# Block-sparse attention with a SwiGLU FFN: one dense batch instead of two, and block batches loaded by GpSimd-issued DMAs

## Chip, cores and metric

The kernel runs on one core of a Trainium2 chip. The metric is the time of one execution in microseconds on the device. The kernel before takes 307.14 us, the median of three runs (306.61 to 308.03). The profile comes from one further execution of 307.95 us, in which 306.2 us lie between the first and the last instruction (the span).

## What is computed

Four batches of eight heads, 768 tokens and head dimension 64 go through attention with a block mask, and the result through a gated FFN. The mask works on blocks of 32 tokens (24 per batch): a query block sees itself and its neighbours, the first and the last block, and three sampled blocks; the first and the last query block see everything.

```python
blk_i, blk_j = pos[:, None] // 32, pos[None, :] // 32
mask = (abs(blk_i - blk_j) <= 1) | (blk_i == 0) | (blk_j == 0) | (blk_i == 23) | (blk_j == 23)
for qb in range(24):
    for kb in sampled_blocks[qb]:
        mask[qb * 32:(qb + 1) * 32, kb * 32:(kb + 1) * 32] = True
attn = softmax(where(mask, q @ k.T / 8, -1e9)) @ v            # [4, 8, 768, 64]
x = attn, heads side by side                                   # [3072, 512]
xn = x / sqrt(mean(x * x) + 1e-6) * rms_g
out = (silu(xn @ w_gate) * (xn @ w_val)) @ w_out               # 512 -> 1536 -> 512
```

## The kernel before

**Two ways of attention.** Batches 0 and 1 are dense: all 768 x 768 scores of a head are computed, with the mask carried by 24 further rows of the contraction (88 = 64 + 24). Batches 2 and 3 are done by blocks: for each tile of four query blocks only the keys and values that the mask allows are gathered and multiplied. The work is cut into units of one to three tiles of 128 tokens (`UNITS`, L59 to L63). Batch 0 has units of 1, 1, 1 and 3 tiles, the others two units of 3. Tile 5 (`AT`) of a block batch holds the first and the last query block, which see everything, with the two blocks before the last.

**A dense unit.** `dk` (L322) computes scores, `dexp` (L343, ScalarE) the exponential, `dav` (L357) multiplies with the values, whose column 65 is ones and gives the row sum, and `dxo` (L369, L370, VectorE) divides by it. Batch 0's queries and keys are turned by TensorE (L301) and batch 1's by DMA transposes (`turn`, L288), after loads by SyncE (`load`, L275) and casts on VectorE (`fill`, `pad_v`).

**A block batch.** SyncE loads raw k, v (`load_kv`, L452, halves of 768 KB with two tokens side by side, in rows of 512 bytes) and q (`load_q`, L459, rows of 256 bytes) into three raw buffers. `fill_v`, `fill_k` and `fill_q` cast them to bf16, on GpSimd for batch 2. `turn_k` (L478) and `turn_q` (L504) are DMA transposes that SyncE issues. `store_v` (L508) writes the bf16 values to DRAM as rows `vrows`. For each tile, `kg_fixed` copies the neighbour and end blocks of the keys and `kg_sampled` (GpSimd, L146) the sampled ones, at columns that registers hold. `pair_v` (L570, L572, L578, SyncE) fetches the fixed value rows. `block_v` (L555) fetches each sampled block of 32 value rows by a DMA of its own: SyncE issues those of the first and second sample, ScalarE those of the third. Then come `qk` (L599) or, for tile 5, `qka` (L615), `exp` (L605) or `expa` (L623), `av` (L648) and `xo` (L658, L659). Registers are loaded once by `table_regs` (L435) on each engine that uses them.

**The FFN of a unit.** `sq`, `rsq` (L686, a power on GpSimd) and `xq` (L693) normalize. Units below `NPET` = 6 are turned by TensorE (`tr`, L704; `cp`), the later ones by a DMA transpose (`xt`, L715). Then for each slice `f` of the hidden dimension TensorE does gate and value (`proj`, L728), ScalarE a tanh (`th`, L737), and VectorE `uu` (L743) and `hp` (L754). TensorE ends with `yy` (L767), ScalarE or VectorE scale (`yo`, L777, L779), and SyncE stores (`so`, L789, L795). Weights come by DMAs that GpSimd issues and that cast to bf16 (`load_w` L248, `load_wo` L252).

**What sets the order.** A planner at the end of the function holds every piece of work as an `op` with a cost for each engine that may do it, dependencies, a priority and the buffers that it takes and gives back. It fixes one order for each engine ahead of time. Each engine then runs its list in order, so an instruction that waits holds up everything after it on its engine. Ops in `seq` keep the order given there. Buffers overlay one another: those of the block batches lie in storage that the dense batches have given back (keys `("old", i)`), so their release sets when block work may begin.

Of the kernel before, what the change touches and what calls it, by code (L numbers as in the profile page):

```python
# [16 lines left out]
def kernel(  # L17
# [32 lines left out]
    NR, NHP, NXN, NYO, NPET = NRND, 2, 2, 3, 6  # L50
    NSLOT, NAUG, NOPEN, NDB = 5, 2, 2, 2
    IXAT, RGAT = 36.0, 48.0
    NPT, NPA, NKG, NVG, NRAW = 4, 2, 2, 3, 3
# [4 lines left out]
    HD = NC * D // 2  # L58
    UNITS = [(0, 0, 1), (0, 1, 1), (0, 2, 1), (0, 3, 3)]  # L59
    UNITS += [(b, c, 3) for b in range(1, NDB) for c in (0, 3)]  # L60
    ND = len(UNITS)
    for b in range(NDB, B):
        UNITS += [(b, (5, 0, 1), 3), (b, (2, 3, 4), 3)]  # L63
    NU = len(UNITS)
    HG = [("h", 0 if u < 3 else u) for u in range(NU)]
    HO = [u if u < 3 else 0 for u in range(NU)]
# [9 lines left out]
    def bank16(n):  # L76
# [12 lines left out]
    VAC = const.tile([P, 2, H * NC, D + 2], BF16, name="VAC")  # L89
    VGC = const.tile([P, 6, VW], BF16, name="VGC")  # L90
# [6 lines left out]
    RAWD = list(A)  # L97
    RAWS = [RAWC[:, i * RB:(i + 1) * RB] for i in range(NRAW)]
    aug = [AUG[:, i] for i in range(NAUG)]
    va_ = [VAC[:, i] for i in range(2)]  # L100
    vfl = [t.rearrange("p m d -> p (m d)")[:, 0:6 * VW] for t in va_]
    VAUG = [t.rearrange("p (t c h d) -> p t c h d", t=NC // 2, c=2, h=H) for t in (vfl[0], PTC[:, 10240:10240 + 6 * VW])]
    rt_ = RAWC[:, NRAW * RB:].bitcast(BF16)
    VGB = [VGC, rt_[:, 0:6 * VW].rearrange("p (x w) -> p x w", w=VW),
           vfl[1].rearrange("p (x w) -> p x w", w=VW)]
    PD = [PTC[:, i * PDW:(i + 1) * PDW] for i in range(3)]
    PTB = [t.rearrange("p (h l x) -> p h l x", h=2, l=2) for t in [rt_[:, 6 * VW:6 * VW + 1024]] + [
        PTC[:, i * 1024:(i + 1) * 1024] for i in range(NPT - 1)]]
    PAB = [PTC[:, 3072 + i * 2048:3072 + (i + 1) * 2048].rearrange("p (l h x) -> p l h x", l=2, h=2) for i in range(NPA)]
    KTB = [t.rearrange("p (a s) -> p a s", a=NP) for t in (xs_[3], xs_[1])]  # L110
    QTB = [t.rearrange("p (a s) -> p a s", a=NP) for t in (xs_[4], PTC[:, 7168:7168 + NP * S])]
    KGB = [xs_[i].rearrange("p (x a s j c) -> p x a s j c", x=6, a=NP, s=4, j=16) for i in (0, 2)]
    KROW = AUG[:, 0].rearrange("p i e c x -> p (i e c x)").rearrange(
        "p (a c t x) -> p a c t x", a=NP, c=2, t=NC // 2)
    QROW = AUG[:, 1].rearrange("p i e c x -> p (i e c x)").rearrange("p (a n x) -> p a n x", a=NP, n=NC)
    kvv = [t.rearrange("b h (t p c) d -> b p (h t) (c d)", p=P, c=2) for t in (k, v)]
    qvv = q.rearrange("b h (n p) d -> b n p h d", p=P)
# [32 lines left out]
    zt = const.tile([P, VW], BF16, name="zt")  # L150
# [36 lines left out]
    nc.gpsimd.memset(zt[0:32, P:VW], 0.0)  # L187
# [9 lines left out]
    for t in va_:  # L197
        nc.vector.memset(t[:, :, D:D + 1], 1.0)
# [72 lines left out]
    def load(g, i):  # L271
        b, pr = divmod(g, NP)
        if i == 0:
            rawd[g] = RAWD[held["rawd", g][1]]
        nc.sync.dma_start(out=rawd[g][:, i], in_=(kv, qv, vv)[i][b, :, 2 * pr:2 * pr + 2, :])  # L275

    def fill(g, i, eng):
        copy(eng, aug[g % NAUG][:, i, :, :, 0:D],
             rawd[g][:, i].rearrange("p h (c d) -> p h c d", d=D))

    def pad_v(g, eng):
        b, pr = divmod(g, NP)
        src = rawd.pop(g) if b else A[g]
        copy(eng, va_[b][:, 2 * pr * NC:2 * (pr + 1) * NC, 0:D],
             src[:, 2].rearrange("p h (c d) -> p (h c) d", d=D))

    def turn(g):
        nc.sync.dma_start_transpose(  # L288
            out=X[g % NSLOT].rearrange("p i e (c t) -> p (i e c) t", t=P),
            in_=aug[g % NAUG].rearrange("p i e c r -> p (i e c r)"))  # L290
# [656 lines left out]
    def dep0(g0, b, c0, nt, kt, g):  # L947
        if b:
            return [("turn", g0)]
# [373 lines left out]
```

## Time and profile before

| | |
|---|---|
| median of the runs | 307.14 us (306.61 to 308.03) |
| the profiled execution, its span | 307.95 us, 306.2 us |
| TensorE busy in matmuls | 284.4 us (93%) |
| VectorE, ScalarE, GpSimd busy | 195.1, 175.2, 80.3 us |
| bytes moved by DMA | 48.50 MB, 158 GB/s over the span |
| packets: all, and under 512 bytes | 85,204 and 48,037 |
| hardware queue of SyncE (q1), share of 16 engines | 54.7% |
| GpSimd's software queue (q0), the same | 10.1% |

A busy time counts the instructions of an engine; registers, semaphores and the issuing of DMAs are not in it and appear under the engine's queue (SPq, ACTq, POOLq). The chain of waits goes back from the last instruction to what released it, step by step; a step on it is work that the end waited for. In a group such as `L728 ... x480 | 74.3, 294`, the numbers are the count, the busy us together and the mean ns of one; then follow the idle time of the engine just before and what ended it.

### The profile page before, as it was taken

The numbers are of one execution on the slowest core, as the hardware profiler recorded it, in microseconds if no ns is written. First come the engines' busy times: TensorE is split into PE (matmuls) and PEld (weight loads), VectorE is DVE, ScalarE is ACT, GpSimd is POOL, SyncE is SP. The second block draws the span as 40 slices with busy tenths as digits, with TensorE's granted clock in tenths as the row PEclk, the third lists the DMA queues.
The fourth block names the chain that finished last, engine by engine and source line by source line (L and its number), as shares of the span: only waits on it lengthen the run. The fifth ranks groups of instructions, "written<-read, shape, count | busy, mean of one in ns | idle before, by whom it ended". The sixth has DMA issues, their size and how long they took to land.

```text
span 306.2 us, 9818 instructions
## 1 busy us (share of the span) xinstructions
PE 284.4 (93%) x3838; PEld 183.4 (60%) x3838; DVE 195.1 (64%) x462; ACT 175.2 (57%) x290; POOL 80.3 (26%) x196
## 2 busy tenths in 40 slices
PE   8999989889999998999779699998699999999995
PEld 7899877666666664665445345564255655546543
DVE  6688896576756755877568435767177958807700
ACT  4899874468888785368554226877065424413322
POOL 4648100010024615119754200755041000100000
PEclk9999999999999999999999979999989999999999
DMA  7999999864799996783987973333754400060032
GB/s 218 364 242 157 203 268 323 182 229 80 119 267 266 182 308 161 159 239 87 263 196 187 195 157 97 90 84 89 166 127 135 92 36 2 0 156 0 1 98 109
DMA packets 85204, 48.50 MB, mean 158 GB/s; under 512 B 48037, under 2 KB 81318, under 8 KB 85158
## 3 DMA queue, kind: packets, MB, share of 16 engines
q1 hardware_dynamic: 76946, 41.63, 54.7%
q0 software_dynamic: 5792, 4.72, 10.1%
q10 hardware_dynamic: 2420, 1.53, 2.0%
q8 instruction: 30, 0.49, 0.6%
q14 instruction: 16, 0.13, 0.1%
HBM read 36.70 MB, written 8.02 MB: 146 GB/s over the span
## 4 chain that ended last, share of the span: by engine, by line
PE 67%; DMA 14%; DVE 8%; issue 5%; SPq 2%; ACT 2%; ACTq 1%; DVEq 0%
PE PS L728 33%; PE PS L767 15%; PE PS L322 7%; PE PS L357 4%; DMA RAWC<-in_v_dram 4%; PE PS L648 3%; DMA XC<-AUG 2%; DMA RAWC<-in_k_dram 2%; PE PS L301 2%; DMA VGC<-vrows 2%; DVE uu L743 2%; PE PS L599 2%; DMA xn<-xq 1%; DVE hp L754 1%; ACT th L737 1%
## 5 line engine op out<-in xcount | busy, mean ns | idle before, releaser
L737 ACT ACTIVATE th<-PS 128x384 bf16<-128x384 f32 x96 | 46.5, 492 | 81.9 <-PE PS L728 37.5
L743 DVE SCALAR_TENSOR_TENSOR uu<-th,PS 128x384 bf16<-128x384 bf16 x96 | 52.4, 551 | 49.4 <-ACT th L737 47.1
L728 PE MATMUL PS<-xn,wg 128*128 128x384 bf16 (+1 forms) x480 | 74.3, 294 | 7.3 <-DVE uu L743 4.2
L343 ACT ACTIVATE PTC<-PS 128x768 bf16<-128x768 f32 x92 | 70.4, 815 | 14.0 <-PE PS L322 13.8
L728 PE MATMUL PS<-xn,wv 128*128 128x384 bf16 (+1 forms) x480 | 77.9, 297 | 0.1
L767 PE MATMUL PS<-wo,hp 128*128 128x512 bf16 (+1 forms) x300 | 71.4, 376 | 4.1 <-DVE uu L743 4.1
L754 DVE TENSOR_TENSOR hp<-uu,PS 128x384 bf16<-128x384 bf16 x96 | 52.0, 551 | 16.8 <-PE PS L728 14.7
L728 PEld LDWEIGHTS <-wg 128*128 128x128 bf16 x480 | 40.7, 98 | 31.4 <-issue 9.0
L146 POOL COPY XC<-XC 128x128 bf16 x132 | 39.3, 371 | 62.6 <-PE PS L599 35.7
L728 PEld LDWEIGHTS <-wv 128*128 128x128 bf16 x480 | 40.5, 98 | 23.9 <-issue 1.9
L767 PEld LDWEIGHTS <-hp 128*128 128x128 bf16 x300 | 29.0, 99 | 32.4 <-issue 6.2
L322 PE MATMUL PS<-XC 88*128 88x128 bf16 (+1 forms) x288 | 42.6, 276 | 0.6 <-ACT PTC L343 0.6
L322 PEld LDWEIGHTS <-XC 88*128 88x128 bf16 x288 | 22.2, 100 | 7.8 <-issue 0.9
L357 PE MATMUL PS<-VAC,PTC 128*128 128x65 bf16 x552 | 21.1, 193 | 0.2 <-DVE XO L370 0.2
L357 PEld LDWEIGHTS <-PTC 128*128 128x128 bf16 x552 | 20.0, 97 | 2.0 <-issue 0.3
L777 ACT ACTIVATE yo<-PS 128x512 f32<-128x512 f32 (+1 forms) x16 | 9.1, 571 | 20.2 <-PE PS L767 20.1
L146 POOL CAST AUG<-RAWC 128x768 bf16<-128x768 f32 (+3 forms) x12 | 11.6, 973 | 30.1 <-DMA RAWC<-in_k_dram 25.7
L693 DVE SCALAR_TENSOR_TENSOR xq<-XO,rs,gB 128x512 bf16<-128x512 f32 x24 | 18.5, 792 | 0.2 <-POOL rs L686 0.2
L686 POOL TENSOR_TENSOR rs<-ms,nhalf 128x1 f32<-128x1 f32 (+1 forms) x6 | 4.3, 714 | 47.8 <-DVE ms L675 47.8
L605 ACT ACTIVATE PTC<-PS 128x1024 bf16<-128x1024 f32 x15 | 15.2, 1022 | 1.6 <-PE PS L599 1.1
L648 PEld LDWEIGHTS <-PTC 128*32 128x32 bf16 x736 | 8.1, 97 | 8.7 <-issue 7.4
L599 PEld LDWEIGHTS <-XC 64*128 64x128 bf16 x480 | 7.5, 93 | 6.9 <-issue 5.8
(112 smaller groups left out, 225.1 us busy)
## 6 DMA issues: line engine op xcount, KB each, us to landing
out_dram<-yo SPq DMA_DIRECT2D x21, 256.0 KB, 2.0
RAWC<-in_k_dram SPq DMA_DIRECT2D x4, 768.0 KB, 5.7
RAWC<-in_v_dram SPq DMA_DIRECT2D x4, 768.0 KB, 10.6
RAWC<-in_q_dram SPq DMA_DIRECT2D x12, 256.0 KB, 5.3
RAWC<-in_v_dram SPq DMA_DIRECT2D x7, 384.0 KB, 6.5
RAWC<-in_k_dram SPq DMA_DIRECT2D x6, 384.0 KB, 6.6
wg<-in_moe_w_gate_dram POOLq DMA_DIRECT2D x4, 384.0 KB, 6.9
wv<-in_moe_w_val_dram POOLq DMA_DIRECT2D x4, 384.0 KB, 7.9
```

The source lines that it names most:

```text
L146: nc.gpsimd.tensor_copy(out=out, in_=in_)
L322: nc.tensor.matmul(out=s_[:, e, j * w:(j + 1) * w], lhsT=x[0:KQ, 0, e, jt * P:(jt + 1) * P], rhs=x[0:KQ, 1, e, c0 * P:c0 * P + w], start=T ...
L343: nc.scalar.activation(out=pts[u, pr][:, g * kt:(g + 1) * kt].rearrange("p j e w -> p e j w"), in_=s_[:, :, 0:kt * w].rearrange("p e (j w) ...
L357: nc.tensor.matmul(out=o_[:, t, e, :], lhsT=pt[:, jt, e, t * P:(t + 1) * P], rhs=va[:, (2 * pr + e) * NC + jt, 0:D + 1], start=(jt == 0), ...
L605: nc.scalar.activation(out=t_.rearrange("p h l x -> p (h l x)"), in_=tiles.pop(("s", b, n, pp)).rearrange("p h l x -> p (h l x)"), func=AF ...
L648: nc.tensor.matmul(out=o_[32 * i:32 * i + 32, a, :], lhsT=l_, rhs=r_, start=i not in begun, stop=k_ == last[i], tile_position=(0, 32 * i), ...
L693: nc.vector.scalar_tensor_tensor(out=xqs[u][:, t, :], in0=xos[u, t].rearrange("p h d -> p (h d)"), scalar=mss[u][:, t:t + 1], in1=gB, op0= ...
L728: nc.tensor.matmul(out=p_[:, j, :].rearrange("p (t w) -> p t w", w=P), lhsT=w_[:, c, f_ * P:(f_ + 1) * P], rhs=xns[u][:, :, c, :], start=( ...
L737: nc.scalar.activation(out=t_, in_=tiles["gp", u, f], func=AF.Tanh, scale=0.5)
L743: nc.vector.scalar_tensor_tensor(out=t_, in0=tiles.pop(("th", u, f)), scalar=1.0, in1=tiles.pop(("gp", u, f)), op0=ALU.add, op1=ALU.mult)
L754: nc.vector.tensor_tensor(out=hps[u][:, f * fg:(f + 1) * fg, :], in0=tiles.pop(("uu", u, f)), in1=tiles.pop(("vp", u, f)), op=ALU.mult)
L767: nc.tensor.matmul(out=tiles["yp", u, t, h], lhsT=hps[u][:, f, t * P:(t + 1) * P], rhs=wo[:, f, x], start=(f == 0), stop=(f == NF - 1))
```

## The change

Batch 1 is done by blocks like batches 2 and 3 (`NDB` 2 to 1), and everything that loaded, cast, turned and multiplied a dense batch above 0 goes. Units of the block batches are 1, 2, 1, 2 tiles in batch 1, 1, 2, 3 in batch 2 and 3, 3 in batch 3; units below 8 are turned by TensorE. The block batches' tokens lie in their natural order: k, v and q are all loaded in halves of 768 KB with rows of 256 bytes, and key copies read runs of 32 neighbouring columns. GpSimd issues these loads, behind the weights. SyncE gathers the first sample of each block, ScalarE the second and the third; their row numbers are packed two to a register. All fixed key copies are VectorE's. There are four value buffers instead of three. Register loads may start at 36 us of the plan (48 before). The core of the diff:

```diff
-    NR, NHP, NXN, NYO, NPET = NRND, 2, 2, 3, 6
-    NSLOT, NAUG, NOPEN, NDB = 5, 2, 2, 2
-    IXAT, RGAT = 36.0, 48.0
-    NPT, NPA, NKG, NVG, NRAW = 4, 2, 2, 3, 3
+    NR, NHP, NXN, NYO, NPET = NRND, 2, 2, 3, 8
+    NSLOT, NAUG, NOPEN, NDB = 5, 2, 2, 1
+    IXAT, RGAT = 31.0, 36.0
+    NPT, NKG, NVG, NRAW = 5, 2, 4, 3
+    SPLIT = (((5,), (0,1), (2,),( 3, 4)), ((5,), (0, 1), (2, 3, 4)), ((5, 0, 1), (2, 3, 4)))
-    UNITS += [(b, c, 3) for b in range(1, NDB) for c in (0, 3)]
-        UNITS += [(b, (5, 0, 1), 3), (b, (2, 3, 4), 3)]
+        UNITS += [(b, ns, len(ns)) for ns in SPLIT[b - NDB]]
...
-    kvv = [t.rearrange("b h (t p c) d -> b p (h t) (c d)", p=P, c=2) for t in (k, v)]
-    qvv = q.rearrange("b h (n p) d -> b n p h d", p=P)
+    kvv = [t.rearrange("b h (t p) d -> b p (h t) d", p=P) for t in (k, v, q)]
...
-    REGS = {"POOL": [("k", 0, 16), ("k", 16, 32), ("k", 32, 2 * NS)], "SP": [("v", 0, 16), ("v", 16, 32), ("v", 32, 2 * NS)],
-            "ACT": [("v", 2 * NS, 2 * NS + 11), ("v", 2 * NS + 11, 3 * NS)]}
+    REGS = {"POOL": [("k", 0, 16), ("k", 16, 32), ("k", 32, 2 * NS)],
+            "DVE": [("k", 0, 16), ("k", 16, 32), ("k", 32, 2 * NS)], "ACT": [("v", 0, 11), ("v", 11, NS)],
+            "SP": [("w", 0, NS // 2)]}
...
+    def piece(x, hi, top):
+        return nc.s_assert_within(x >> 10 if hi else x & (HALF - 1), 0, top, skip_runtime_bounds_check_because=WHY)
+    def v_at(n, r):
+        return piece(*((regs["SP", "w", n % (NS // 2)], n >= NS // 2) if r == 0 else (regs["ACT", "v", n], r == 2)), 32 * (NB + 1))
...
     def load_kv(b, i, hf):
-        key = ("kv"[i], b, hf)
+        key = ("kvq"[i], b, hf)
         raws[key] = RAWS[held["raw", key][1]]
-        nc.sync.dma_start(
-            out=raws[key].rearrange("p (x y) -> p x y", y=2 * D),
-            in_=kvv[i][b, :, 3 * HH * hf:3 * HH * (hf + 1), :])
-
-    def load_q(b, n):
...
+        nc.gpsimd.dma_start(
+            out=raws[key].rearrange("p (x y) -> p x y", y=D),
+            in_=kvv[i][b, :, NC * HH * hf:NC * HH * (hf + 1), :])
...
     def kg_sampled(b, n, xs, eng):
-        kg = new_kg(b, n).rearrange("p x a s j c -> p x a c s j")
-        kt = KTs[b].rearrange("p a (c y) -> p a c y", c=2)
+        kg = new_kg(b, n)
         for x, r in xs:
-            kb = k_at(blocks(n)[x] - 1, r)
-            copy(eng, kg[:, x, :, :, r, :], kt[:, :, :, bass.ds(kb, 16)])
+            copy(eng, kg[:, x, :, r, :], KTs[b][:, :, bass.ds(k_at(blocks(n)[x] - 1, r, eng), 32)])
...
-    def block_v(b, n, x, r):
-        (nc.scalar if r == 2 else nc.sync).dma_start(
-            out=new_vg(b, n)[32 * r:32 * r + 32, x, :],
-            in_=vrows[b][bass.ds(voff[(blocks(n)[x] - 1) * NR + r], 32), :])
+    def block_v(g, n, x, r):
+        (nc.scalar if r else nc.sync).dma_start(
+            out=new_vg(g, n)[32 * r:32 * r + 32, x, :],
+            in_=vrows[g][bass.ds(v_at(blocks(n)[x] - 1, r), 32), :])
...
-    CE = {2: {"POOL": 1.0}, 3: {"DVE": 0.62, "ACT": 0.86, "POOL": 1.0}}
-    QE = {2: {"POOL": 1.5}, 3: {"DVE": 1.4, "ACT": 1.47, "POOL": 1.5}}
+    KDV, LIC = 0.48, 1.5
+    CE = {1: (P_,D_,D_), 2: (AP_,AP_,AP_), 3: (AP_,AP_,AP_)}
+    KFE, SQE, YOE = ("DVE",), ("DVE", "ACT"), ("DVE", "ACT")
+    KDE, CPE = ("POOL", ), ("DVE", "ACT")
...
-    seq += [("ld", g, i) for g in range(2 * NP - 1, NDB * NP) for i in range(3)]
-    for b in range(NDB, B):
-        kv_ = [("l", x, b, hf) for x in ("kv" if b == NDB else "vk") for hf in range(2)]
-        seq += kv_ + [("lq", b, n) for n in range(NC)]
+    seq += first[at_:]
+    seq += [("li", x, b, hf) for b in range(NDB + 1, B) for x in ORD for hf in range(2)]
...
-    for g in range(NP, NDB * NP):
-        b, pr = divmod(g, NP)
...
-        op(("turn", g), {"SP": 1.0}, [("fill", g, 0), ("fill", g, 1)], (-1, g),
-           lambda e, p, g=g: turn(g), [(f"X{g % NSLOT}", g)], [(f"aug{g % NAUG}", (g, False))], d=4.6)
...
-                op(("l",) + key, {"SP": 0.8}, pv01, (1,), lambda e, p, a=(b, i, hf): load_kv(*a), [("raw", key)], d=2.8)
+                op(("li",) + key, {"POOL": LIC}, [("wi", NWC - 1, 1)], (1,), lambda e, p, a=(b, i, hf): load_kv(*a), [("raw", key)])
+                op(("l",) + key, {"GQ": 3.0}, [("li",) + key], (1,), None)
...
-                op(("gv",) + T + (x,), {"SP": 2 * GVC}, [("st", b)] + rgs["SP", "v"], (GVP, order, x),
-                   lambda e, p, a=T + (x,): [block_v(*a, r) for r in range(2)], [("vg", T)], d=0.2)
+                for x in xs[::2]:
+                    op(("gv",) + G + (x,), {"SP": 2 * GVC}, sts + rgs["SP", "w"], (GVP, order, x),
+                       lambda e, p, a=G, x=x: [block_v(*a, x_, 0) for x_ in (x, x + 1)], [("vg", T)], d=0.2)
+                for x in xs:
+                    op(("gw",) + G + (x,), {"ACT": 2 * GVC}, sts + rgs["ACT", "v"], (GWP, order, x),
+                       lambda e, p, a=G + (x,): [block_v(*a, r) for r in (1, 2)], [("vg", T)])
```

## The prediction

> **What bounds the kernel now.** I read the page first, then the table by stage, the chain of waits and ScalarE's waits.
>
> ```profile
> span 306.2 us, 9818 instructions
> PE 284.4 (93%) x3838; PEld 183.4 (60%) x3838; DVE 195.1 (64%) x462; ACT 175.2 (57%) x290; POOL 80.3 (26%) x196
> PE   8999989889999998999779699998699999999995
> PEclk9999999999999999999999979999989999999999
> PE 67%; DMA 14%; DVE 8%; issue 5%; SPq 2%; ACT 2%; ACTq 1%; DVEq 0%
> ```
>
> TensorE is busy for 284.4 of 306.2 us and holds 67% of the chain, so what changes its work changes the time, unless the change also changes its 21.8 us of idleness. Where that idleness lies is told by the stages (columns: stretch, its length, PE, PEld, DVE, ACT, POOL busy us with counts, clock, DMA share, GB/s):
>
> ```profile
> 45.00:105.00 60.00, 57.99 (x651) 39.85 (x651) 41.05 (x89) 42.01 (x65) 9.00 (x11) 1.00 0.93 206
> 105.00:155.00 50.00, 46.10 (x809) 28.50 (x806) 33.32 (x76) 32.23 (x50) 23.07 (x62) 1.00 0.81 202
> 155.00:200.00 45.00, 40.14 (x495) 22.07 (x496) 25.87 (x56) 22.34 (x45) 15.28 (x45) 0.96 0.66 154
> 200.00:240.00 40.00, 35.09 (x726) 19.70 (x725) 25.39 (x58) 21.02 (x37) 13.09 (x40) 0.96 0.46 114
> 240.00:306.00 66.00, 62.97 (x479) 34.97 (x477) 34.27 (x70) 21.11 (x43) 1.11 (x2) 1.00 0.20 55
> ```
>
> From 45 to 105 us, batch 1's dense stage, TensorE idles 2.0 us. From 105 to 240 us, the block stage of batches 2 and 3, it idles 3.9 + 4.9 + 4.9 = 13.7 us, and the clock of 0.96 in two stretches takes 0.04 x 85 = 3.4 us more: 17.1 us for 12 block tiles.
>
> **TensorE's work.** The rate of each matmul comes from the chain, where a group's length is its pitch:
>
> ```profile
> 66.08 0.67 PE PS L728 x12
> 66.75 0.65 PE PS L322 x4
> 68.08 0.65 PE PS L767 x3
> 71.43 1.14 PE PS L357 x36
> ```
>
> Removed: batch 1's dense scores, 2 units x 4 pairs x 12 = 96 matmuls at 0.65/4, 15.6 us; its attention times values, 288 at 1.14/36, 9.1 us. Added: one batch by blocks. Two batches show 9.8 + 3.1 + 12.6 us busy for L599, L615 and L648 (the lines' own rows by stage), 12.7 a batch with pipeline ends counted in; by pitch in TensorE's timeline (24 of L599 in 0.42, 32 of L648 in 0.34, 18 of L615 in 0.36, the long values step 64 in 0.83) it is 5 x 1.52 + 1.44 + 1.66 = 10.7. I take the middle, 11.7. Batch 1's FFN goes from two units of 384 columns to widths 128, 256, 128, 256: at 0.67/12 for 128 and the straight line between 128 and 384 for 256, 192 matmuls of 128 and 192 of 256 cost 31.7 us against 31.3, so +0.4. The output matmuls and transposes keep their number. Sum: -15.6 - 9.1 + 11.7 + 0.4 = **-12.6 us** (-13.6 to -11.6).
>
> **The start of batch 1.** Batch 0's FFN is 288 gate and value matmuls of 128 columns, 96 of 384 and 72 of output: 16.1 + 15.6 + 15.6 = 47.3 us. By 45 us the lines' rows by stage show 132 of the narrow ones done (7.4 us), 34 of 48 wide scores, 216 of 288 values and 12 of 24 transposes. Left: 39.9 + 2.3 + 2.3 + 0.8 = 45.3 us, so cover reaches to about 90 us. Batch 1's loads queue on GpSimd behind wo, which lands between 43 and 50 us (13.7 and 20.0 us after its issues). Natural order makes every row 256 bytes. The nearest stretches are one with only q loads (256 bytes) and one with only v loads (512):
>
> ```profile
> 100.00:105.00 5.00, 5.00 (x37) 2.84 (x34) 4.60 (x9) 3.48 (x5) 3.26 (x4) 1.00 1.16 184
> 110.00:115.00 5.00, 5.00 (x60) 3.37 (x59) 2.75 (x6) 3.63 (x6) 0.00 (x0) 1.00 1.17 302
> ```
>
> At 184 GB/s a half (786 KB) takes 4.3 us, six take 26: the last q lands near 76, two fills (0.6 each) and a transpose (7.8 to landing, the row of PTC<-AUG) bring scores to about 85 us. Hidden, with 5 us of margin. The Trainium skill, "DMA: Bandwidth & Descriptors", section "Issuing engines are not separate DMA queues", speaks against a gain in bandwidth: loads from any engine run on the same 16 DMA engines. The table agrees that rows, not issuers, set the rate: 184 against 302 GB/s at equal share. Batches 2 and 3 pay 1.7 us more for each of 8 k and v halves, beside 60 us of TensorE work a batch: hidden.
>
> GpSimd's price for such an issue isn't in the trace; the weights have 512 to 768 rows against 3,072 here:
>
> ```profile
> L248 POOL DMA_DIRECT2D wg<-in_moe_w_gate_dram x4: 788/806/1149, 13.3 to 27.6; - x4
> L252 POOL DMA_DIRECT2D wo<-in_moe_w_out_dram x2: 845/846/848, 29.2 to 30.0; - x2
> ```
>
> From 512 to 768 rows nothing grows, so the low end is 0.85 us; in proportion to rows it is 5.0. I take 1.5, nearer to the flat rows: 18 issues, 27 us (15 to 90) on an engine 26% busy. At 5.0 the margin of 5 us goes and copies of sampled keys (L146, 0.37 each, 132 now, 198 then) queue behind each issue. The fourth to sixth load of a batch also wait, on GpSimd, for one of three raw buffers to be emptied; behind them stand those copies and the powers (L686) that xq waits for. Before, GpSimd's fills waited 25.7 us for k loads and no TensorE gap followed, so I price it at nothing; uncovered, it is one fill and one landing, 4 us a batch. The Trainium skill, "SBUF — State Buffer", section "SBUF: two separate sides", warns that a VectorE copy in its fast mode locks GpSimd out of writing descriptors, 620 ns becoming 3,100. Here the two issues between 15.95 and 17.64 us ran beside casts of VectorE (14.76 to 16.46 and from 16.78) at 0.82 and 0.88 us, not five times as long; by the page's factor an issue of 1.5 us would be 7.5, the 18 135 us, and the loads late.
>
> **SyncE and VectorE.** SyncE loses 12 loads, 4 dense transposes and batch 2's and 3's k, v and q loads, whose issues held it up to 5.9 us for two; it gains one batch's transposes, store and gathers. So its queue is freer; what that gains is unknown, 0 to 3 us of the 17.1, and I take none. VectorE loses 12 fills and pads (7.3), two memsets (0.9), 8 normalizing pairs (6.0); it gains 12 pairs (7.2), all fixed key copies of three batches (about 19 more) and fills (4): 195 to about 211 us of 299, no bound.
>
> **ScalarE's queue, where I see the danger.** Sampled value rows are gathered by L555. ScalarE issued one row block in three, now two: 22 a batch become 44, over three batches 132 instead of 44. Each takes 0.5 us (three in 1.51). Behind them stands the next tanh (L737), which uu, hp and TensorE's next gate matmuls need.
>
> ```profile
> 168.81 0.48 ACT L737 ACTIVATE th<-PS 128x384 bf16<-128x384 f32 x1
> 169.28 5.66 ACTq L555 DMA_DIRECT2D VAC<-vrows  x3
> 175.04 0.87 ACT L737 ACTIVATE th<-PS 128x384 bf16<-128x384 f32 x2 [5.75 <-DMA XC<-AUG]
> ```
>
> Three issues took 5.66 us while SyncE issued a transpose, and TensorE then stood 3.03 us until 176.6. In all, 21.3 us of tanh waits stand behind these 44 issues. Against that ScalarE loses 48 exponentials of 0.815 (39.1), gains 10 of 1.02 and 4 of 1.03 (14.3), and gives 11.5 us of key copies away: 175 + 22 of issues become 139 + 66, still 205 of 299. Its total is no bound; its blocked stretches are. A third block batch scales the 17.1 us to 25.7, +8.6, if nothing improves; below, 0 if freer queues pay for it. I take the middle, +4.3. The register loads (L435, 4.1 and 5.4 us on ScalarE) move to between 36 and 50 us, where exponentials fill ScalarE; they cost TensorE 0.8 + 0.9 us at 54 and 62; I take +1.0 (0 to 7.8, their full length).
>
> **The sum.** -12.6 + 4.3 + 1.0 = -7.3: span 298.9. The profiled execution took 307.95 with a span of 306.2, so 300.6 in its own terms; the median of 307.14 lies 0.8 lower: **299.8 us**.
>
> **Rivals.** (a) *Full gain*: block idleness does not grow, because loads leave SyncE's queue and four value buffers replace three. For: SyncE's loads were in the chain for 11.4 and 6.7 us. Against: most of the 13.7 us ended on ScalarE or transposes, which stay. 307.1 - 12.6, or - 15.6 with 3 us from the freer queue: 291.5 to 294.5. (b) *ScalarE's gathers hold the tanh*, ending slower: 88 more issues, in the block stage, each set able to stand behind a transpose. Of the 17.1 us the gaps of 1.2 us at 121 and 3.0 at 174, with one clock dip of 1.7, belong to them: 5.9 us for 44 issues, 17.7 for 132, +11.8; with the other 11.2 us scaled to 16.8, +5.6, and registers +1.0, less 12.6, the net is +5.8: 313. It decides once the added idleness passes 12.6 us, 0.7 for each of 18 tiles. Against: ScalarE is emptier by 36 us of busy time. (c) *The loads come late*, that is, issuing from GpSimd doesn't free anything: at 5 us an issue the margin is gone and three batches come 2 to 4 us late each: 299.8 + 6 to 12, 306 to 312; at 1 us late each it is 303.
>
> **Chances.** Forecast (296 to 304) 0.42; (a) 0.22; (b) 0.20; (c) 0.16, spread as 0.04 faster, 0.06 same, 0.06 slower. Within 0.5% (1.5 us) is about what this measurement can tell from no change. Faster 0.42 + 0.22 + 0.04 = 0.68, same 0.06, slower 0.20 + 0.06 = 0.26. The range runs from (a) with a little more to the middle of (b): 290 to 311.
>
> **What would show it.** TensorE's busy time near 272. No TensorE gap near 85 to 95 us, else the margin failed. GpSimd's load issues near 1.5 us. Idleness and clock loss per block tile near 1.2 us (17.1 + 4.3 over 18); tanh waits behind L555 under 45 us in all (21.3 for 44 issues would be 64 for 132); no issue of several us for a load on SyncE. Wrong would be TensorE busy over 277, or idle over 34 us, the present 21.8 and 12.6 more.

## The result and the profile after

The changed kernel takes **361.27 us** (360.03 to 367.61) against 306.88 us of the kernel before, measured beside it: a ratio of 1.177, 95% interval 1.168 to 1.185. One of its four runs, the 367.61 us, was in a slower state, and the ratio goes by the other three. The prediction was 299.8 us with a range of 290 to 311 us. The profiled execution took 360.03 us. Its page:

```profile
span 358.3 us, 11538 instructions
...
PE 281.3 (79%) x4466; PEld 193.8 (54%) x4502; DVE 206.6 (58%) x503; ACT 136.9 (38%) x222; POOL 126.0 (35%) x298
...
PEclk9999997898666988995559999999999999999999
...
q1 hardware_dynamic: 46434, 28.30, 36.1%
q0 software_dynamic: 9536, 18.88, 26.9%
...
PE 50%; DMA 30%; DVE 4%; issue 4%; ACT 3%; ACTq 3%; POOL 2%; SPq 2%; POOLq 0%; DVEq 0%
```

TensorE's share of the chain fell from 67 to 50%, and DMA's rose from 14 to 30%. TensorE is busy 3.1 us less than before and idle 77.0 us instead of 21.8, so idleness alone added 55.2 us. The clock row has dips to 5 and 6 that the page of before does not have. The table by stage, in the columns of the prediction, shows where:

```profile
45.00:75.00 30.00, 24.10 (x296) 18.85 (x299) 14.99 (x31) 9.44 (x16) 11.46 (x11) 0.89 0.87 214
75.00:115.00 40.00, 19.06 (x91) 9.20 (x91) 13.76 (x30) 3.48 (x8) 11.90 (x24) 0.74 1.02 157
115.00:150.00 35.00, 26.26 (x686) 16.12 (x683) 19.96 (x52) 16.36 (x24) 18.36 (x54) 0.90 0.68 169
150.00:190.00 40.00, 17.25 (x308) 13.63 (x307) 12.39 (x31) 7.38 (x13) 13.08 (x21) 0.66 1.03 143
190.00:250.00 60.00, 51.17 (x1147) 38.83 (x1156) 41.44 (x87) 24.70 (x37) 34.28 (x93) 1.00 0.69 164
250.00:358.00 108.00, 102.01 (x1289) 61.05 (x1301) 69.56 (x151) 40.23 (x73) 17.40 (x58) 1.00 0.27 76
```

Two stretches of 40 us, from 75 to 115 and from 150 to 190, hold 20.9 and 22.8 us of idleness. In both the DMA engines are busy throughout (1.02 and 1.03 of their time, by the packets' durations) and yet move only 157 and 143 GB/s, less than the 214 GB/s of the stretch before. The chain of waits names what was moved there:

```profile
79.58 20.06 DMA XC<-AUG
99.64 12.19 DMA VXC<-AUG
...
154.94 27.82 DMA XC<-AUG
```

These are the transposes of batch 1's keys and queries and of batch 2's keys, from issue to landing: 60.1 us of the chain. In SyncE's timeline the six key and query transposes take long while loads run, and are quick only for batch 3, the last two:

```profile
79.58 19.95 SPq L464 DMA_TRANSPOSE XC<-AUG  x1
99.64 9.32 SPq L469 DMA_TRANSPOSE VXC<-AUG  x1
...
154.94 11.18 SPq L464 DMA_TRANSPOSE XC<-AUG  x1
...
172.56 12.36 SPq L469 DMA_TRANSPOSE XC<-AUG  x1
...
233.73 5.39 SPq L464 DMA_TRANSPOSE XC<-AUG  x1
...
244.28 3.63 SPq L469 DMA_TRANSPOSE VXC<-AUG  x1
```

Before, such transposes took 3.65 to 4.45 us in the block stage. GpSimd's timeline shows the next batch's loads going out just ahead of the first of them and beside it:

```profile
75.97 1.47 POOL L447 DMA_DIRECT2D RAWC<-in_v_dram  x1 [4.98 <-DVE AUG L152]
78.67 1.57 POOL L447 DMA_DIRECT2D RAWC<-in_v_dram  x1 [1.23 <-DVE AUG L152]
80.23 1.42 POOL L447 DMA_DIRECT2D RAWC<-in_k_dram  x1
...
87.16 1.42 POOL L447 DMA_DIRECT2D RAWC<-in_k_dram  x1 [0.41 <-POOL PTC L150]
```

How this reaches TensorE is read from ScalarE's timeline and waits. ScalarE's gathers stand in its list before a tanh (L699); while they cannot go out, the tanh waits, uu (L705) waits for it, and TensorE's next gate matmuls (L690) wait for uu: 45.0 us in 10 waits. So batch 0's FFN, the work that was to cover the start of batch 1, stood still too.

```profile
85.38 12.57 ACTq L517 DMA_DIRECT2D PTC<-vrows  x4
98.05 0.87 ACT L699 ACTIVATE th<-PS 128x384 bf16<-128x384 f32 x2 [12.46 <-DMA PTC<-vrows]
99.22 9.31 ACTq L517 DMA_DIRECT2D PTC<-vrows  x4
...
183.23 0.60 ACT L699 ACTIVATE th<-PS 128x512 bf16<-128x512 f32 x1 [25.02 <-DMA XC<-AUG]
```

A row of the timeline merges neighbours: `12.57 ... x4` is four gathers with the waits between them. No single gather took ScalarE more than 1.64 us to issue (minimum, median and maximum in ns), but some took long to land:

```profile
L517 ACTq DMA_DIRECT2D VXC<-vrows x72: 322/323/1639, 71.8 to 298.6; - x72
L517 ACTq DMA_DIRECT2D PTC<-vrows x60: 322/322/1272, 79.9 to 285.5; - x60
...
DMA to landing us min/median/max: 1.6/2.4/16.6
```

What the gathers waited for stands in the trace's records of semaphores (counters by which an instruction learns that another is done). Each DMA of SyncE and of ScalarE reports its landing on one of eight semaphores, which the two engines share, and 333 of these 342 DMAs wait for their own semaphore, that is, for the DMA that used it before. The gathers issued at 93.11 and 97.63 us had waited 6.7 and 4.0 us until gathers issued at 79.89 and 80.98 us landed. The gather at 182.79 us had waited 25.0 us until the key transpose issued at 154.94 us landed, though it reads no keys. Such waits of over 0.3 us before ScalarE's gathers come to 75 us; in the kernel before they are 13 us.

### The profile page after: what moved, and what is told of

The parts are those of the page before. It is cut to its first block, busy times and chain, and to the rows that moved or that the text cites. A ratio compares the mean times of both kernels' runs of the same rounds, so it can differ in the third digit from the quotient of the medians.

```text
span 358.3 us, 11538 instructions
## 1 busy us (share of the span) xinstructions
PE 281.3 (79%) x4466; PEld 193.8 (54%) x4502; DVE 206.6 (58%) x503; ACT 136.9 (38%) x222; POOL 126.0 (35%) x298
## 3 DMA queue, kind: packets, MB, share of 16 engines
q0 software_dynamic: 9536, 18.88, 26.9%
## 4 chain that ended last, share of the span: by engine, by line
PE 50%; DMA 30%; DVE 4%; issue 4%; ACT 3%; ACTq 3%; POOL 2%; SPq 2%; POOLq 0%; DVEq 0%
PE PS L690 25%; DMA XC<-AUG 13%; PE PS L729 13%; DMA RAWC<-in_k_dram 5%; DMA VXC<-vrows 5%; DMA VXC<-AUG 3%; PE PS L610 3%; DMA PTC<-vrows 3%; ACTq L517 3%; PE PS L561 3%; PE PS L305 2%; PE PS L340 2%; ACT PTC L326 2%; SPq L517 1%; PE PS L284 1%
## 5 line engine op out<-in xcount | busy, mean ns | idle before, releaser
L690 PE MATMUL PS<-xn,wg 128*128 128x128 bf16 (+2 forms) x624 | 78.3, 274 | 46.5 <-DVE uu L705 45.0
L699 ACT ACTIVATE th<-PS 128x384 bf16<-128x384 f32 (+1 forms) x90 | 45.1, 512 | 152.9 <-PE PS L690 65.9
L705 DVE SCALAR_TENSOR_TENSOR uu<-th,PS 128x384 bf16<-128x384 bf16 (+1 forms) x90 | 51.5, 578 | 73.8 <-ACT th L699 72.0
L690 PEld LDWEIGHTS <-wg 128*128 128x128 bf16 x624 | 51.3, 101 | 67.5 <-issue 52.2
L690 PE MATMUL PS<-xn,wv 128*128 128x128 bf16 (+2 forms) x624 | 81.5, 275 | 7.9 <-DVE hp L716 7.9
L150 POOL COPY XC<-XC 128x128 bf16 x198 | 51.3, 310 | 59.6 <-DMA XC<-AUG 44.1
L690 PEld LDWEIGHTS <-wv 128*128 128x128 bf16 x624 | 50.6, 101 | 28.1 <-issue 11.3
L716 DVE TENSOR_TENSOR hp<-uu,PS 128x384 bf16<-128x384 bf16 (+1 forms) x90 | 51.4, 577 | 21.7 <-PE PS L690 20.0
L326 ACT ACTIVATE PTC<-PS 128x768 bf16<-128x768 f32 x44 | 33.0, 819 | 4.9 <-PE PS L305 4.8
L152 DVE COPY XC<-XC 128x256 bf16<-128x256 bf16 (+1 forms) x63 | 18.3, 337 | 8.8 <-DMA XC<-AUG 8.5
L610 PEld LDWEIGHTS <-PTC 128*32 128x32 bf16 x1056 | 12.1, 99 | 20.7 <-issue 8.4
L305 PE MATMUL PS<-XC 88*128 88x128 bf16 (+1 forms) x192 | 21.3, 245 | 0.8 <-ACT PTC L326 0.6
L150 POOL CAST AUG<-RAWC 128x768 bf16<-128x768 f32 (+2 forms) x17 | 14.0, 846 | 7.0 <-DMA RAWC<-in_q_dram 5.8
L621 DVE TENSOR_TENSOR XO<-PS,rz 128x256 f32<-128x256 f32 x36 | 15.3, 424 | 1.2
L447 POOL DMA_DIRECT2D RAWC<-in_v_dram x6 | 8.9, 1479 | 17.3 <-DVE uu L705 11.1
## 6 DMA issues: line engine op xcount, KB each, us to landing
RAWC<-in_k_dram POOLq DMA_DIRECT2D x6, 768.0 KB, 15.9
```

Source lines behind the costliest of these rows:

```text
L150: nc.gpsimd.tensor_copy(out=out, in_=in_)
L152: nc.vector.tensor_copy(out=out, in_=in_)
L305: nc.tensor.matmul(out=s_[:, e, j * w:(j + 1) * w], lhsT=x[0:KQ, 0, e, jt * P:(jt + 1) * P], rhs=x[0:KQ, 1, e, c0 * P:c0 * P + w], start=T ...
L326: nc.scalar.activation(out=pts[u, pr][:, g * kt:(g + 1) * kt].rearrange("p j e w -> p e j w"), in_=s_[:, :, 0:kt * w].rearrange("p e (j w) ...
L610: nc.tensor.matmul(out=o_[32 * i:32 * i + 32, a, :], lhsT=l_, rhs=r_, start=i not in begun, stop=k_ == last[i], tile_position=(0, 32 * i), ...
L690: nc.tensor.matmul(out=p_[:, j, :].rearrange("p (t w) -> p t w", w=P), lhsT=w_[:, c, f_ * P:(f_ + 1) * P], rhs=xns[u][:, :, c, :], start=( ...
```

## The experiments

**Theory 1**: GpSimd's uncast loads run in large packets. The after page shows it: q0 moved 18.88 MB in 9,536 packets, and the packets of the loads have 4,096 bytes and take 302 ns on average, though a row is 256 bytes. The transposes run in packets of 256 bytes, 22 ns each where they are alone. The theory: where both queues have work, the engines take packets in turn, so the transposes and gathers get little and land late. Counted per 5 us in the trace, the transposes of 85 to 100 us got 358 to 605 packets; alone, in the bench below, they get some 3,700. **Rivals**: the number of ScalarE's gathers; GpSimd as the issuer, with its order and waits; the missing cover of batch 1 by blocks; the bytes, not the packets.

**e1: loads on SyncE.**

```diff
-        nc.gpsimd.dma_start(
+        nc.sync.dma_start(
             out=raws[key].rearrange("p (x y) -> p x y", y=D),
```

> One part undone: the block batches' loads are issued by SyncE again, everything else as in the changed kernel, the written order too. Theory 1 (GpSimd's loads run as packets of about 4 KB and share the DMA engines packet by packet with the transposes' 256-byte packets, so the transposes of k and q take 9 to 20 us to issue and ScalarE's gathers and SyncE stand behind them): transposes back to 4 to 6 us each, the idle TensorE stretches near 90 to 109 and 159 to 185 us gone, 312 to 325 us. Theory 2 (ScalarE's 132 gathers hold the tanh whatever the transposes do): at least 345 us, stretches of several us stay. Theory 3 (batch 1 by blocks has too little FFN work as cover): at least 335 us, TensorE idle between 75 and 135 us as before.

Measured 349.4 us (1.135, interval 1.116 to 1.155). The transposes of batch 1 fell to 4.09 and 7.62 us, the others to 3.6 to 6.6 us. Theory 1's 312 to 325 us were missed. SyncE is now held up by an issue, in an order that was planned without it: the issue of one k half alone held it for 16.9 us. TensorE still idles 60 us. So this run shows the quicker transposes and little of the time.

**e2: casting loads.** The raw buffer is viewed as bf16, so the load writes half the bytes, and the fills read bf16.

```diff
-        raws[key] = RAWS[held["raw", key][1]]
+        raws[key] = RAWS[held["raw", key][1]].bitcast(BF16)[:, 0:RB]
```

> The loads stay on GpSimd but cast to bf16 on the way, so that each row of 64 becomes 128 bytes; the weights, which cast, ran in packets of one row each (750 bytes and 1 KB). Values are rounded to bf16 in the load instead of in the copy behind it. Theory 1: packets of one row each no longer hold the transposes up, these fall to 4 to 8 us each and the time to 312 to 330 us; with packets still of several KB nothing changes. Were it enough that two queues are in use, whatever the packets: transposes still 9 us and more, 350 us and more. Theories 2 and 3: 350 us and more.

Measured 332.9 us (1.082, 1.068 to 1.096), 28 us less from one line. The software queue's line and two transposes, from the page and SyncE's timeline:

```profile
q0 software_dynamic: 61376, 11.80, 43.0%
```

```profile
76.84 8.45 SPq L464 DMA_TRANSPOSE XC<-AUG  x1
85.41 8.71 SPq L469 DMA_TRANSPOSE VXC<-AUG  x1
```

Casting loads run row by row: six times the packets. The first transpose fell from 19.95 to 8.45 us, and it is still twice as long as in the kernel before. The time is a little above theory 1's 312 to 330 us. The cast changes two things at once, packets and bytes; m2 below takes them apart.

**e3: fewer gathers on ScalarE.** SyncE gathers the second sample, as it gathers the first; ScalarE issues 66 instead of 132.

```diff
-        (nc.scalar if r else nc.sync).dma_start(
+        (nc.scalar if r == 2 else nc.sync).dma_start(
```

> One part undone: the second sample's value rows are gathered by SyncE again, so ScalarE issues 66 gathers instead of 132 in the three block batches, at most 4 a tile. Theory 2: 20 us or more come back, under 341 us. Theory 1: transposes stay at 9 to 20 us, and one gather behind such a transpose is enough to hold ScalarE, so 345 to 362 us. Theory 3: 350 to 362 us.

Measured 381.8 us (1.241, 1.226 to 1.255): slower than the changed kernel, and than any theory expected. With half the gathers, one tanh still waited 25.6 us, while two transposes in SyncE's queue took 29.3:

```profile
ACT th L699 <- issue: 25.6, 1, 25.6
```

```profile
73.73 15.22 SPq L464 DMA_TRANSPOSE XC<-AUG  x1
89.06 14.04 SPq L469 DMA_TRANSPOSE VXC<-AUG  x1
```

The rival of the number falls. A single gather is enough: the one before this tanh waited 25.0 us until the key transpose issued at 73.73 us had landed, since it has the same semaphore. That SyncE's queue now has more to hold up may be why the time rose; no run shows it.

**e4: the kernel before, with its block loads on GpSimd.** Batch 1 stays dense.

```diff
-        nc.sync.dma_start(
+        nc.gpsimd.dma_start(
             out=raws[key].rearrange("p (x y) -> p x y", y=2 * D),
```

> One part alone: the kernel before (two dense batches, 512-byte rows of k and v), with the k, v and q loads of its two block batches issued by GpSimd. Theory 1: transposes that meet a load take 8 us or more instead of 3.6 to 4.5, and the time rises to 315 to 340 us. Theory 3 (the block treatment of batch 1 is at fault): 305 to 311 us. Theory 2: 305 to 311 us, since ScalarE's gathers are as before.

Measured 329.6 us (1.071, 1.061 to 1.081): this part alone, on two batches, costs 22 us. TensorE stood 14.3 us from 87.6 us on, waiting for a transpose of dense batch 1 (7.92 us to issue, before 4.30). So the missing cover of block batch 1 is not needed for the loss.

**e4c: the same with casting loads.**

> The kernel before with batches 2 and 3 loaded by GpSimd-issued DMAs that cast to bf16 on the way (the raw values are rounded in the load instead of in the fill). With uncast loads from GpSimd it took 329.6 us against 307.1. Theory 1: with packets of one row instead of 4 KB the transposes issue in 4 to 6 us and most of the 22 us comes back: 308 to 316 us. Rival (what costs is that GpSimd issues them, in its order and with its waits for raw buffers): 325 to 332.

Measured 313.1 us (1.023, 1.017 to 1.029). Of the 22 us, 16 to 17 came back with issuer and order unchanged; some 6 us are left with GpSimd issuing the loads, and were not taken apart.

**e5: keys and queries turned by TensorE**, in the changed kernel: transposes through PSUM in place of the two DMA transposes of each block batch, with evictions on VectorE and ScalarE.

```diff
-            op(("turn" + x, b), {"SP": 1.0}, ...
+            for pr in range(NP):
+                op(("t" + x, b, pr), {"PE": 6 * 0.056}, ...
+                op(("e" + x, b, pr), {"DVE": 0.56, "ACT": 0.8}, ...
```

> The changed kernel, with k and q of the block batches turned by TensorE (48 transposes a batch, 3 us, with 8 copies out of PSUM on VectorE or ScalarE) instead of by DMA; GpSimd's loads stay as they are. Theory 1 (transposes held up by the loads' packets, and gathers and tanh behind them): with no such transpose to be held up, no tanh wait over 5 us behind a gather, 305 to 322 us. Theory 3 (too little cover for batch 1 by blocks): the load still ends when it ended, TensorE idles between 75 and 135 us, 335 us or more. Theory 2 (number of gathers on ScalarE): 335 us or more.

Measured 328.2 us (1.069, 1.060 to 1.078): 33 us of the 54 are gone with the DMA transposes, though TensorE does 144 more transposes. That is more than theory 1's 305 to 322 us and less than the 335 of the others.

**e5c: e5 with e2's casting loads.**

> As the run with TensorE's transposes, and the loads cast to bf16 on the way (small packets, half the bytes written). Theory 1: the gathers that are left also meet smaller packets, 0 to 10 us below the run without the cast, 300 to 315 us. Theories 2 and 3: 325 us or more.

Measured 306.3 us (0.996, 0.990 to 1.002). The page's rows:

```profile
span 302.7 us, 11877 instructions
...
PE 281.5 (93%) x4646; PEld 196.8 (65%) x4646; DVE 214.4 (71%) x522; ACT 142.4 (47%) x224; POOL 126.9 (42%) x301
...
PE 62%; DMA 16%; DVE 7%; issue 4%; SPq 3%; ACTq 3%; ACT 2%; POOL 1%; POOLq 0%; DVEq 0%
```

TensorE is back at 93% with 132 gathers on ScalarE, GpSimd issuing all loads and batch 1 by blocks. So neither the gathers' number, nor GpSimd as issuer, nor too little cover costs the 54 us. Casting takes 22 us off even where no key or query transpose by DMA is left; so the uncast loads cost something else too. Whether they hold up other DMAs (gathers, stores, transposes of the FFN) or land later themselves (a k half in 9.7 us against 7.0, median) was not told apart.

**e6: turns and loads kept apart.** SyncE's turns wait for both fills, and a batch's k and q loads wait on GpSimd until the batch before is turned.

```diff
+            if b > NDB and (i, hf) == (1, 0):
+                for t_ in (KTs[b - 1], QTs[b - 1]):
+                    nc.gpsimd.tensor_copy(out=scf, in_=t_[:, NP - 1, S - 1:S])
...
+        nc.sync.dma_start(out=scr[0:1, 12:14], in_=QROW[0:1, NP - 1, 0, 0:2])
```

> The changed kernel with loads and k and q transposes kept apart: the k transpose starts only when the batch's q is cast, and GpSimd starts the next batch's loads only when both transposes have landed. Packets and counts stay. Theory 1: each k and q transpose takes 3.6 to 4.5 us, tanh waits behind gathers fall under 30 us in all; the loads come later, so 320 to 340 us, below the 361 us without the gate. Theory 2: tanh waits as before, 355 us or more. Theory 3: later loads mean less cover, 365 us or more.

Measured 338.4 us (1.103, 1.092 to 1.112). All six transposes now issue in 3.91 to 4.19 us, as theory 1 said, and the time lies in its 320 to 340 us:

```profile
88.05 4.13 SPq L468 DMA_TRANSPOSE XC<-AUG  x1
92.24 4.19 SPq L473 DMA_TRANSPOSE VXC<-AUG  x1
```

The first starts 8.5 us later than in the changed kernel, and GpSimd's copies wait 58.0 us for the keys instead of 44.1. Keeping the two apart makes the transposes quick and the data late.

**e7 and e7p: loads cut into even and odd rows**, so that rows that follow each other are no longer neighbours in the buffer; e7 in the changed kernel, e7p in e5.

```diff
+        for c in range(2):
+            nc.gpsimd.dma_start(
+                out=raws[key].rearrange("p (x c y) -> p c x y", c=2, y=D)[:, c], ...
```

> The changed kernel with each load of the block batches cut into two issues, one for the even and one for the odd rows of 256 bytes, so that rows that follow each other no longer lie side by side in the raw buffer. Bytes, type, engine and order stay; GpSimd issues 36 loads instead of 18. Theory 1 (the loads run in large packets, and a transpose of 256-byte packets gets one packet in turn with them): if the packets become single rows, the software queue shows near 75,000 packets instead of 9,536, SyncE's transposes take 4 to 9 us to issue instead of 9 to 20, and the time falls to 325 to 345 us; if rows are packed whether or not they are neighbours, packets and transposes stay as they are and the time with them, 355 to 370. Rival (what helped in the kernel with casting loads is that they write half the bytes, and packet size is nothing): the packets may shrink, but the bytes are the same, so the transposes still take 9 to 20 us and the time stays at 355 to 370.

> The same cut of the loads in the kernel whose keys and queries are turned by TensorE (328.2 us with whole loads, 306.3 with casting loads), so that no transpose by DMA of keys or queries is left. Theory 1: with packets of one row the gathers, stores and transposes of the FFN no longer wait behind packets of 4 KB, and the time falls most of the way to the casting kernel: 306 to 316 us. Rival (bytes, not packets): 326 to 334, or more by the 18 further issues on GpSimd, 25 us of an engine that is not the bound.

e7 measured 356.0 us (1.160, 1.153 to 1.168), and the software queue still shows 9,824 packets: rows are packed whether they are neighbours or not. The cut did not make small packets, so these two runs don't tell packets from bytes. e7p measured 321.1 us (1.050, 1.043 to 1.057), 7 us better than e5 with the same packets. That was not expected of either theory, and its cause stays open.

**m1 and m2: the disputed cost by itself.** Benches without attention and FFN, whose output is zeros: SyncE issues two transposes of 128x3072 bf16, alone or beside three loads of 3,072 rows of 256 bytes. In m1 two stages have small DMAs on ScalarE too. In m2 ScalarE issues the same uncast loads, which its hardware queue moves row by row.

> No attention and no FFN is computed, the output is zeros: six stages with a full wait between them measure two DMA transposes of 128 x 3,072 bf16 by themselves. (1) alone; (2) beside three GpSimd loads of 768 KB in fp32; (3) beside three such loads that cast to bf16; (4) behind three loads on SyncE's own queue; (5) as 2, with five small DMAs issued by ScalarE; (6) as 1 with the same five. Theory 1: 3.6 to 4.5 us a transpose in 1 and 6, 10 us or more in 2 and 5, between these in 3, and ScalarE's copy behind its DMAs waits in 5 until the transposes are issued (10 us or more) and in 6 about 5. If loads beside a transpose only share bandwidth: at most twice the time in 2 and 5.

> The bench again (it computes no attention and no FFN, and writes zeros), with six stages, each of two transposes of 128x3072 bf16 by SyncE: alone; beside three uncast fp32 loads of 3,072 rows of 256 bytes issued by GpSimd; beside the same three loads issued by ScalarE, on its hardware queue; beside casting loads by GpSimd; then the ScalarE stage and the uncast GpSimd stage again. In the first bench the two transposes took 7.8 us to issue alone, 23.2 beside uncast and 15.8 beside casting loads. Theory 1 (packets): ScalarE's loads move the same bytes of the same type, but in packets of 256 bytes, so the transposes take 10 to 17 us beside them, like beside casting loads; and the uncast GpSimd stages give 22 to 24 again. Rival (bytes): 22 to 25 us beside ScalarE's loads as beside GpSimd's, since the bytes are the same.

SyncE's timeline of m1: alone, beside uncast loads of GpSimd, beside casting ones, behind SyncE's own loads (the last two stages, with the small DMAs, took 22.64 us beside uncast loads and 7.54 alone):

```profile
18.77 7.83 SPq L104 DMA_TRANSPOSE xt<-row  x2
...
31.91 23.16 SPq L104 DMA_TRANSPOSE xt<-row  x2
...
60.36 15.77 SPq L104 DMA_TRANSPOSE xt<-row  x2
...
85.96 11.67 SPq L104 DMA_TRANSPOSE xt<-row  x2
```

Of m2: beside uncast loads of GpSimd, the same loads of ScalarE, casting ones, ScalarE's and GpSimd's uncast ones again:

```profile
31.90 20.66 SPq L110 DMA_TRANSPOSE xt<-row  x2
...
56.40 12.15 SPq L110 DMA_TRANSPOSE xt<-row  x2
...
78.26 16.29 SPq L110 DMA_TRANSPOSE xt<-row  x2
...
98.44 11.62 SPq L110 DMA_TRANSPOSE xt<-row  x2
...
119.97 23.22 SPq L110 DMA_TRANSPOSE xt<-row  x2
```

The same bytes of the same type cost the transposes 12 us in packets of 256 bytes (18,528 packets for 4.72 MB on ScalarE's queue) and 21 to 23 us in packets of 4,096. Nor is it the rate: while the transposes ran, ScalarE's loads moved 127 to 132 GB/s and GpSimd's uncast ones 100 to 112. The rival of the bytes falls, and theory 1 stands as far as these two go. Packet size isn't all, though: casting loads, in packets of 128 bytes and at 72 to 74 GB/s, cost the transposes 16 us, more than ScalarE's. What else GpSimd's queue or the cast adds stays open.

One part of m1's expectation missed: beside the slow transposes ScalarE's four gathers went out in 1.93 us. Yet two of them, whose landing the trace tells, landed 15.9 and 16.2 us after their issue, against 2.4 and 4.6 us beside the same transposes without loads. So the bench shows gathers landing late beside the loads; ScalarE went on because no further DMA of its own stood behind them for the same semaphores, as in the kernel.

**e8: batch 3 turned by DMA again**, in e5c, since no load follows it.

```diff
-        for x in "kq":
+        for x in "kq" if b < B - 1 else "":
             for pr in range(NP):
```

> The kernel with casting loads and keys and queries turned by TensorE (306.3 us), but with batch 3, the last, turned by DMA transposes again, since no load follows beside which they could run. Theory 1: TensorE loses 48 transposes by 128 columns and 8 evictions go, some 2.7 us, and the two transposes issue in 3.6 to 5 us as they did in the other kernels (3.63 to 5.39 us for this batch): 302 to 305 us. Rival (a DMA transpose of the block stage costs in itself, through the wait of a ScalarE gather behind it or because batch 3's loads are still running): 306 to 312.

Measured 311.4 us (1.016, 1.010 to 1.022): in the rival's range. The transposes are quick (4.13 and 4.45 us), but ScalarE's timeline shows six gathers held for 5.8 us and the tanh behind them for 10 us, and TensorE stands 2.9 us from 179 us on:

```profile
174.91 5.81 ACTq L528 DMA_DIRECT2D PTC<-vrows  x6
180.83 0.49 ACT L710 ACTIVATE th<-PS 128x384 bf16<-128x384 f32 x1 [10.00 <-issue]
```

The rival's reason isn't shown by it. The two longest waits of these gathers, 2.5 and 1.5 us, were for output stores issued at 170.8 and 171.2 us, before the first of the two transposes went out at 175.8 us. And of the 8.9 us that TensorE idles more than in e5c, 3.6 lie between 170 and 185 us and 4.6 between 200 and 250 us. Why e8 is slower stays open.

**e9: e5c with each casting load in two neighbouring halves.**

```diff
+        for c in range(2):
+            lo = NC * HH // 2 * c
+            nc.gpsimd.dma_start(
+                out=raws[key].rearrange("p (x y) -> p x y", y=D)[:, lo:lo + NC * HH // 2], ...
```

> The kernel with casting loads and keys and queries turned by TensorE (306.3 us), with each load cut into two issues of neighbouring halves, as the cut loads of the uncast kernel took 7 us off it (321.1 instead of 328.2). If that gain came from the gaps between shorter transfers, in which other DMAs get their turn, 300 to 305 us here. Rival (with packets of one row the other DMAs have their turn already, so the cut brings only 18 more issues of 1.4 us on GpSimd): 306 to 310 us.

Measured 306.5 us against 307.4 (0.994, 0.989 to 0.999): no different from e5c, and at the edge of what is faster than the kernel before.

## Why the prediction was wrong

**The start of batch 1 is the step that failed.** It put a transpose at "7.8 to landing", scores at "about 85 us" and called the loads "Hidden, with 5 us of margin". The loads kept their time: the last q half landed at 73.1 us, with 76 forecast, and the k transpose was issued at 79.6 us. It then took 20.1 us to land, and the q transpose, issued behind it, 12.2 more: 111.8 us. The sum had one transpose after the last load; the 7.8 us were those of batch 3's queries in the kernel before, with other neighbours on the DMA engines. The next batch's loads, issued between 76 and 89 us, stood in no term of it: they were priced as transfers that have to be hidden, not as neighbours of the transpose. The same holds for "Batches 2 and 3 pay 1.7 us more": batch 2's k transpose took 27.8 us to land. That the loads are the reason is shown by e2, e4c, e5, e5c and m2.

**The cover failed with it.** The step let batch 0's FFN reach to 90 us whatever the DMAs did. In the run ScalarE's gathers waited for late landings, and the tanh of that FFN behind them: TensorE did 19.1 us of work from 75 to 115 us.

**The rule weighed was read too narrowly.** "Issuing engines are not separate DMA queues" holds here in bandwidth: in the two bad stretches the engines are full. But the step concluded that rows, and not the issuer, set the rate. (Its row from 110 to 115 us, read as v loads alone, also holds 1,024 packets of 256 bytes and 184 of about 2 KB beside 1,694 of 512, so its 302 GB/s isn't the rate of 512-byte rows.) On GpSimd the 256-byte rows no longer travelled one by one. The same page, the Trainium skill, "DMA: Bandwidth & Descriptors", has the other half in the section "🔬 Queues, rings and completion order": an engine goes round its queues packet by packet. Another section, "🔬 SWDGE vs HWDGE vs iDMA", says that a packet is up to 4,096 bytes by preference. The traces agree on the size (4,096 bytes a packet for uncast loads of GpSimd) and on the effect (20.7 to 23.2 us against 11.6 to 12.2). As the profile counts packets, the sharing is not one for one: in m2, from 35 to 50 us, 318 to 824 packets of the transposes went through in 5 us beside 94 to 152 large ones.

**TensorE's work**, -12.6 us, held in kind, a little too large. (The sum left out that batch 2's units change too, from 3 and 3 tiles to 1, 2 and 3; at its own rates that is +0.2 us.) e8 against e5c prices a transpose at 2.4 us for 48, 0.05 each, so e5c without its 144 would be busy 274.3 us: an estimate of -10.1 against 284.4, short of the -11.6 at which the term's range ends. The busy time "near 272" was not seen in the changed kernel, which shows 281.3, some 7 us more than this estimate at a mean clock of 0.914 instead of 0.989. The two bad stretches have 0.74 and 0.66. So of 52.1 us of added span, -10.1 is work, about +7 goes with the lower clock (argued, since no run holds the clock alone), and +55.2 is idleness.

**Idleness, +4.3 us**, was the scaled middle of 17.1 us and became +55.2. Scaling by tiles assumed transposes and gathers that land as before.

**ScalarE's gathers**: the prediction saw the place, "each set able to stand behind a transpose", and priced it by their number. It read "Three issues took 5.66 us" off a merged row: none of the three took more than 0.90 us, and the third waited 3.5 us until the k transpose issued at 167.34 us had landed, which had its semaphore. So the price is the time to landing of the DMA that used the semaphore before, of either engine. That time grew: gathers landed within 6.2 us before and 16.6 now, and batch 2's k transpose in 27.8. Tanh waits behind L517 were 51.9 us, over the 45 set as a limit, and the 25.0 us behind the k transpose come on top. e3 shows that the number isn't the price.

**The issue price of 1.5 us** was right (L447, minimum, median and maximum in ns):

```profile
L447 POOL DMA_DIRECT2D RAWC<-in_v_dram x6: 1416/1473/1567, 43.6 to 156.3; - x6
L447 POOL DMA_DIRECT2D RAWC<-in_k_dram x6: 1418/1428/1479, 46.5 to 194.6; - x6
```

The fivefold issue, worked out from the Trainium skill, "SBUF — State Buffer", section "SBUF: two separate sides", is seen in none of these 18 issues; the longest, 1.57 us at 78.7 us, began beside casts of VectorE that ran from 76.3 to 79.2 us.

**The wait for raw buffers, priced at nothing**, was 5.4 us on GpSimd before the first q load; no run prices it alone. TensorE's gap of 5.4 us from 54.7 us on has another reason: the first k half landed 12.1 us after its issue, and VectorE's cast of it stood before the uu that TensorE waited for. That is the prediction's "one fill and one landing, 4 us", uncovered. In e5c 2.6 us of this gap is left.

**SyncE's queue, "freer"**: the opposite. Its six key and query transposes took 61.8 us to issue. Before, the four of the block batches took 16.3 us and the four of dense batch 1 17.9.

**The register loads, +1.0**: they began at 43.1 and 46.2 us on ScalarE (2.4 to 2.7 us each), before the first large gap. GpSimd's first two (3.8 and 3.6 us, from 35.6 us on) stood before its first load, which went out at 43.6 us. No run priced them alone.

**What the change would bring without these loads** is shown by no run. e5c, at the time of the kernel before, pays an estimated 7.2 us for its 144 transposes on TensorE.

## What to carry to other kernels

Moving a load to another engine can also change its packets and who shares the DMA engines with it: look up bytes per packet of each queue, and check which transfers of small packets are needed while the large ones run. Price a transfer by its neighbours after the change, not by its row before it. When an engine both issues DMAs and feeds the critical path, ask of each DMA what it has to wait for before it goes out: here it was the landing of an earlier DMA, of either engine, that reported on the same semaphore. And a merged row of a timeline isn't the length of one issue: look at the minimum, median and maximum too.

## What the hardware showed

- GpSimd's uncast loads of 256-byte rows ran in packets of 4,096 bytes, also where the rows weren't neighbours in SBUF (9,536 and 9,824 packets in all on its queue); the same loads with a cast to bf16 ran in packets of 128 bytes (61,376).
- Two transposes of 128x3072 took 7.8 us to issue alone, 12 beside row-sized packets of another hardware queue, 16 beside casting loads and 21 to 23 beside packets of 4,096 bytes. In m2 such a large packet took 275 ns on average just before the transposes began to move (30 to 35 us), 379 and 704 in the next two stretches of 5 us beside them, and 220 in the third.
- An issue of 3,072 rows took GpSimd 1.42 to 1.57 us, against 0.74 to 1.15, mostly near 0.8, for 512 to 768 rows.
- ScalarE's three loads of 3,072 rows took 0.42, 2.44 and 7.81 us to issue in m2, one after the other; GpSimd issued the same second and third in 2.8 us. A queue that is still full of rows would explain it; that is not shown.
- Gathers of 32 rows landed in 2.4 and 4.6 us beside two transposes, and in 15.9 and 16.2 us beside the same transposes and uncast loads of GpSimd (m1).
